# Last value tiles stored behind the next loads, their splits cut in threes, the last two steps taken product by product

## The chip, the core and the metric

The kernel runs on one core of a Trainium2 chip. The metric is device time in microseconds (us), the median of several runs. Engines: PE is TensorE (matmuls), DVE is VectorE, ACT is ScalarE, POOL is GpSimd, SP is SyncE, which here issues every DMA. Each engine works through its own list in order; it waits where an operand is not there yet, and all that stands behind in its list waits with it.

## What is computed

A chain of three parts. Attention over inputs of shape (4, 8, 576, 64), one branch downsampled by four and one masked to a band of width seven, added. Then two dense blocks over 2304 tokens. The second of these is what the change touches:

```python
def _moe2_ref(x, w_gate, w_val, w_out):     # (2304,512) x (512,1536), twice; then (1536,512)
    gate = 1.0 / (1.0 + np.exp(-(x @ w_gate)))
    val = x @ w_val
    return (gate * val @ w_out).astype(np.float32)
```

## The kernel before

Every fp32 product is three matmuls (`mm3`, lines 292 to 294): each operand is split in a high part, a copy rounded to the matmul type that ACT makes (`copy`, line 302), and a low part, the rest that DVE makes by a subtraction. The matmuls are high x high, high x low (of the moving operand), low (of the weight) x high. Tokens go in six chunks of 384, taken as three pairs p. Matrix products of the second block are made by a seven-product scheme on 2 x 2 quarters (`PRODUCTS`, `order_b`): seven matmul products on sums and differences of quarters instead of eight.

**The stage that ends at about 797 us** (lines 1180 to 1206) runs over six column groups j, three pairs p and two sides (side 0 the gate, side 1 the value). After each product PE goes on and `ends_of` lets ACT copy (`one`, `two`, `three`) and DVE add PSUM banks into tiles `c`; DVE then multiplies value by gate (line 1024). The product u goes to memory as seven forms (`u_sums`, lines 987 to 1007): b11 and the tile `low` (b21, b22) by two stores that SP issues at once (997, 998), and four differences that POOL subtracts (line 1000), stored by `stores()` some ticks later. A tick is a step of the program that lays the instructions out; a deferred call is written into the lists that many ticks later, so ticks set the order in each engine's list, and data decides when it runs.

**The last stage** (lines 1243 to 1269) makes six passes, each over six steps i; a step takes seven products of u forms by output weight forms, 21 matmuls. Its data come back from memory: u forms by `u_fetch` (line 1074), weights by `w_fetch` (1051). During the last column group (j = 5) three generators, `first_w`, `first_u` and `first_splits`, already fetch what the first pass needs, into tiles as the value stage lets them go: u forms in `pieces` of one to five forms of 384 columns, and they split them (`u_hi` on ACT, `u_lo` on DVE, line 1080; `w_hi`, `w_lo`, line 1059, for weights). How fast these splits are laid out between the value stage's own work is set by `rate` (credit per tick, line 1187) and by the price that a generator yields (line 1178). Names in rows: `x<-u` and `f<-u` are loads of u forms into tiles freed by the value stage, `f<-o` the weights of steps 4 and 5, `o<-o` weights of other steps, `u<-u` the eight last u forms, `u<-c` and `u<-t` stores of the value tiles and their differences.

**The end of a pass** is `out_ends` (line 1219): ACT copies the first sum, DVE adds the six others (line 981) into four tiles, and each finished tile goes out by a store (`put`, line 1227); in the last pass the last tile goes out in two halves.

Of the kernel before, what the change touches and what calls it, by code (L numbers as in the profile page):

```python
# [33 lines left out]
N = 384  # L34
# [6 lines left out]
NJ = F2 // 2  # L41
# [23 lines left out]
def tile_kernel(ctx: ExitStack, tc: tile.TileContext, qk, vp, v, w1, w2, mask, ident, out):  # L65
# [52 lines left out]
    def defer(n, fn, *args):  # L118
        events.setdefault(now[0] + n, []).append((fn, args))
# [10 lines left out]
    def run_later(kind=None, age=0):  # L130
        for x in list(waiting):
            if now[0] >= x[0] + age and kind in (None, x[1]):
                waiting.remove(x)
                x[2]()
# [7 lines left out]
    def run_chains(todo):  # L142
        while todo:
            for g in list(todo):
                if next(g, True):
                    todo.remove(g)

    def tick():
        now[0] += 1
        run_chains(chains.pop(now[0], []))  # L150
        todo = events.get(now[0], [])
        while todo:
            fn, args = todo.pop(0)
            fn(*args)
        events.pop(now[0], None)
        run_later(age=8)
        if beat[0]:
            beat[0]()
        lanes_step()

    lanes, credit, rate = [], [0.0], [0.0]

    def lanes_step():

        credit[0] = min(credit[0] + rate[0], 1.5)
        busy = True
        while lanes and credit[0] > 0 and busy:
            busy = False
            for lane in list(lanes):
                if lane[1] is not None and not lane[1]():  # L170
                    continue
                lane[1] = None
                got = next(lane[0], None)
                if got is None:
                    lanes.remove(lane)
                elif callable(got):
                    lane[1] = got
                else:
                    credit[0] -= got
                busy = True  # L180
                if credit[0] <= 0:
                    break

    def lane(g):
        lanes.append([g, None])

    def after(n):
        at = now[0] + n
        return lambda: now[0] >= at
# [101 lines left out]
    def mm3(o, wh, wl, xh, xl, first, last, **kw):  # L291
        nc.tensor.matmul(out=o, lhsT=wh, rhs=xh, start=first, stop=False, **kw)  # L292
        nc.tensor.matmul(out=o, lhsT=wh, rhs=xl, start=False, stop=False, **kw)  # L293
        nc.tensor.matmul(out=o, lhsT=wl, rhs=xh, start=False, stop=last, **kw)  # L294
# [6 lines left out]
    def copy(dst, src):  # L301
        nc.scalar.activation(out=dst, in_=src, func=ACTF.Copy)  # L302
# [5 lines left out]
    def store(dst, src):  # L308
        nc.sync.dma_start(out=dst, in_=src)
# [447 lines left out]
    while any(((1, 0), k) not in xt for k in range(KD)):  # L757
        keep_warm(2)
        if started[0] < n_first:
            x = items[started[0]]  # L760
# [226 lines left out]
    def u_sums(j, p, top, low, last, after_copy):  # L987
        if after_copy:
            nc.gpsimd.tensor_copy(out=spare_sb, in_=mark[after_copy][:, :1])

        if 2 in formed:
            t1, t2, t3 = (wpools["xs"].tile([128, N], F32, tag="xs", name="t") for _ in range(3))
        else:
            t1, t2, t3 = gates[0][:, 0, :], gates[0][:, 1, :], gates[1][:, 0, :]
        b11, b12, b21, b22 = top[:, 0, :], top[:, 1, :], low[:, 0, :], low[:, 1, :]
        to = ud[p][:, j]
        store(to[:, 0, :], b11)
        store(to[:, 1:3, :], low)
        for out, a, b in ((t1, b12, b11), (t3, b22, b12), (t2, b22, t1), (b12, b21, t2)):
            nc.gpsimd.tensor_tensor(out=out, in0=a, in1=b, op=ALU.subtract)  # L1000

        def stores():
            for at, t in ((3, t1), (5, t3), (4, t2), (6, b12)):
                store(to[:, at, :], t)
            summed_u.add((j, p))

        defer(4 if last else 1, stores)
# [35 lines left out]
    w_sets, u_forms, groups, w_room = {}, {}, [], {}  # L1043
# [9 lines left out]
    def w_hi(key):  # L1053
        t = w_room[key]
        copy(t[:, 0], t[:, 1].bitcast(F32))
# [6 lines left out]
    def pieces(i):  # L1062

        n, todo, at = 7 * i, 7, 0
        for g in list(groups):
            size = g[0].shape[1]
            if n < size and todo:
                k = min(size - n, todo)
                yield at, [x[:, n:n + k, :] for x in g]
                at, todo, n = at + k, todo - k, size  # L1070
            n -= size

    def u_fetch(p, i, at, t):
        nc.sync.dma_start(out=t[1].bitcast(F32), in_=ud[p][:, i, at:at + t[1].shape[1], :])

    def u_hi(t):
        copy(t[0], t[1].bitcast(F32))
# [79 lines left out]
    def first_splits():  # L1157

        p = 0
        done = set()  # L1160
        while len(u_forms) < 7 * NJ or len(fetched_w) < 8 or any(("w", x) not in done for x in fetched_w):
            ready = [(t, "u", x) for x, t in fetched_u.items() if ("u", x) not in done]
            ready += [(t, "w", x) for x, t in fetched_w.items() if ("w", x) not in done]
            ready = [x for x in ready if now[0] >= x[0] + 6]
            if not ready:
                yield after(1)
                continue
            _, kind, x = min(ready)
            done.add((kind, x))
            if kind == "w":  # L1170
                w_hi(x)
                defer(2, w_lo, x)
                yield 1.05
            else:
                t = dict(pieces(x[0]))[x[1]]
                u_hi(t)
                defer(2, u_lo, p, *x, t)
                yield 0.2 + 0.4 * t[0].shape[1]

    for j in range(NJ):  # L1180
        for p in range(len(PAIRS)):
            cycle[:] = now[0], p
            for side in range(2):
                while (j, side) not in form or p not in formed:
                    rate[0] = 0.9
                    tick()
                rate[0] = 1.0 if j == NJ - 1 else 0.4 if side else 0.65
                w = form[j, side]
                ends = ends_of(j, side, p)
                bank = next(ends)  # L1190
                if (j, p, side) == (NJ - 1, 0, 0):
                    for g in (first_w(), first_u(), first_splits()):
                        lane(g)
                for n, (a, b, at) in enumerate(PRODUCTS):
                    for k in range(2):
                        x = xform[p, k, b]
                        wh, wl = (w[:, i, a, 128 * k:128 * k + 128] for i in range(2))
                        mm3(
                            bank[at], wh, wl, x[:, 0, :], x[:, 1, :], n < 4 and k == 0,
                            k == 1, skip_group_check=n > 3,  # L1200
                        )
                    defer(1, next(ends))
                    tick()
                if p == len(PAIRS) - 1:
                    made.add((j, side))
                made.add((j, side, p))

    order_b = [(A11, B11), (S2, T2), (S1, T1), (S3, T3), (A12, B21), (S4, B22), (A22, T4)]
    passes = [(0, 0), (0, 1), (1, 1), (1, 0), (2, 0), (2, 1)]
# [33 lines left out]
    rate[0] = 0.9  # L1243
    for q, (p, e) in enumerate(passes):
        ends = None
        for i in range(NJ):
            while (e, i) not in w_sets or any((p, i, a) not in u_forms for a in range(7)):
                tick()
            w = w_sets[e, i]
            if i == 0:  # L1250
                banks = [sum_bank() for _ in range(7)]
            for n, (a, b) in enumerate(order_b):
                x = u_forms[p, i, b]
                mm3(banks[n][:, :N], w[:, 0, a], w[:, 1, a], *x, i == 0, i == NJ - 1)
                if i == NJ - 1:
                    ends = ends or out_ends(q, banks)
                    defer(1, next, ends)
                if n % 2 or n == 6:
                    tick()
            if q + 1 < len(passes) and q % 2 == 0 and i < 4:  # L1260
                key, wait = (1 - e, (i + 2) % NJ if q == 0 else i), 10 if q == 0 else 1
                defer(wait, w_fetch, key, w_room[e, i])
                defer(wait + 10, w_hi, key)
                defer(wait + 12, w_lo, key)
            if q % 2 and q + 1 < len(passes):
                for k, (at, t) in enumerate(pieces(i)):
                    u_fetch(p + 1, i, at, t)
                    defer(10 + k, u_hi, t)
                    defer(12 + k, u_lo, p + 1, i, at, t)
# [70 lines left out]
```

## Time and profile before

| | us |
|---|---|
| median of three runs | 942.21 (941.45 to 948.34) |
| the profiled execution | 942.37 |
| its span, first to last instruction | 940.6 |
| PE busy in it | 917.7 (98%) |
| DVE busy | 591.9 (63%) |
| ACT busy | 466.0 (50%) |
| POOL busy | 184.1 (20%) |

Between the span and the time of the execution lie 1.8 us that no instruction covers. PE is busy nearly throughout, so what a change can gain has to be sought in the short stretches in which PE stands still or steps slowly, and at the end behind its last matmul. In the timeline, a line gives start and duration, the engine and source line, what is written from what, the count of merged instructions, and in brackets the idle time before it and who ended that. Instructions of DVE and of ACT overlap their neighbours by some 0.08 us; PE's matmuls overlap by half, so PE is read by the distance from start to start.

### The profile page before, as it was taken

The numbers are of one execution on the slowest core, as the hardware profiler recorded it, in microseconds if no ns is written. First come the engines' busy times: TensorE is split into PE (matmuls) and PEld (weight loads), VectorE is DVE, ScalarE is ACT, GpSimd is POOL, SyncE is SP. The second block draws the span as 40 slices with busy tenths as digits, with TensorE's granted clock in tenths as the row PEclk, the third lists the DMA queues.
The fourth block names the chain that finished last, engine by engine and source line by source line (L and its number), as shares of the span: only waits on it lengthen the run. The fifth ranks groups of instructions, "written<-read, shape, count | busy, mean of one in ns | idle before, by whom it ended". The sixth has DMA issues, their size and how long they took to land.

```text
span 940.6 us, 16697 instructions
## 1 busy us (share of the span) xinstructions
PE 917.7 (98%) x6368; PEld 879.8 (94%) x6368; DVE 591.9 (63%) x993; ACT 466.0 (50%) x1161; POOL 184.1 (20%) x200
## 2 busy tenths in 40 slices
PE   7889999999999999999999999999999999899998
PEld 7678889999999999999999999999999999799997
DVE  6698965334433533466775587777768668668581
ACT  4767765544543544443644455353434356356440
POOL 2244130302222020000023243323132332200000
PEclk9899999999999999999999999999999999999999
DMA  8357553202223120357441225343425367887960
GB/s 299 126 184 271 181 166 115 65 29 78 91 64 90 44 74 20 132 227 266 149 143 45 93 101 176 124 166 118 157 110 174 113 210 252 279 311 250 327 204 35
DMA packets 72433, 142.50 MB, mean 152 GB/s; under 512 B 6608, under 2 KB 58400, under 8 KB 68000
## 3 DMA queue, kind: packets, MB, share of 16 engines
q1 hardware_dynamic: 72352, 141.43, 44.2%
q8 instruction: 50, 0.82, 0.4%
q14 instruction: 31, 0.25, 0.1%
HBM read 97.76 MB, written 43.65 MB: 150 GB/s over the span
## 4 chain that ended last, share of the span: by engine, by line
PE 88%; DVE 5%; DMA 3%; ACT 2%; issue 1%; SPq 0%; POOLq 0%; POOL 0%; DVEq 0%; ACTq 0%
PE acc L292 13%; PE ab L292 13%; PE acc L293 13%; PE acc L294 13%; PE ab L293 13%; PE ab L294 13%; PE ab L537 2%; PE ab L528 2%; PE ab L457 1%; PE ab L426 1%; DMA u<-c 1%; PE acc L753 1%; PE ab L374 1%; DMA raw<-in_w 1%; PE ab L408 1%; DVE w L263 1%
## 5 line engine op out<-in xcount | busy, mean ns | idle before, releaser
L305 DVE TENSOR_TENSOR t<-ab,t 128x384 f32<-128x384 f32 x94 | 52.3, 556 | 139.3 <-ACT t L655 138.8
L292 PE MATMUL ab<-x,w 128*128 128x384 f32 x376 | 131.5, 350 | 2.6 <-DVE t L305 2.5
L292 PE MATMUL acc<-g,w 128*128 128x384 f32 x384 | 133.2, 348 | 0.0
L293 PE MATMUL acc<-g,w 128*128 128x384 f32 x384 | 130.2, 339 | 0.0
L294 PE MATMUL acc<-g,w 128*128 128x384 f32 x384 | 129.9, 338 | 0.0
L294 PE MATMUL ab<-x,w 128*128 128x384 f32 x376 | 127.2, 338 | 0.1
L293 PE MATMUL ab<-x,w 128*128 128x384 f32 x376 | 127.0, 338 | 0.0
L655 ACT ACTIVATE t<-ab 128x384 f32<-128x384 f32 x94 | 46.1, 491 | 134.8 <-PE ab L294 132.6
L292 PE MATMUL ab<-x,f 128*128 128x384 f32 x261 | 88.3, 338 | 2.6 <-ACT f L302 2.6
L294 PE MATMUL ab<-x,f 128*128 128x384 f32 x261 | 88.4, 339 | 1.7 <-DVE f L1059 1.7
L292 PE MATMUL acc<-x,f 128*128 128x384 f32 x261 | 88.3, 338 | 1.2 <-DVE two L981 1.0
L293 PE MATMUL ab<-x,f 128*128 128x384 f32 x261 | 88.1, 338 | 0.0
L294 PE MATMUL acc<-x,f 128*128 128x384 f32 x261 | 87.7, 336 | 0.0
L293 PE MATMUL acc<-x,f 128*128 128x384 f32 x261 | 87.6, 336 | 0.0
L305 DVE TENSOR_TENSOR g<-t,g 128x384 fp32r<-128x384 f32 x96 | 56.1, 585 | 40.4 <-ACT g L302 38.6
L292 PEld LDWEIGHTS ab<-x,w 128*128 128x128 f32 x376 | 71.1, 189 | 5.5 <-DVE t L305 2.8
L292 PEld LDWEIGHTS acc<-g,w 128*128 128x128 f32 x384 | 72.5, 189 | 2.2 <-issue 1.2
L293 PEld LDWEIGHTS acc<-g,w 128*128 128x128 f32 x384 | 72.7, 189 | 0.6 <-issue 0.4
L302 ACT ACTIVATE g<-t 128x384 fp32r<-128x384 f32 x96 | 50.1, 523 | 46.1 <-DVE t L305 46.0
L294 PEld LDWEIGHTS acc<-g,w 128*128 128x128 f32 x384 | 72.6, 189 | 0.1
L294 PEld LDWEIGHTS ab<-x,w 128*128 128x128 f32 x376 | 71.1, 189 | 0.6 <-DVE w L263 0.5
L293 PEld LDWEIGHTS ab<-x,w 128*128 128x128 f32 x376 | 71.2, 189 | 0.1
(186 smaller groups left out, 2038.6 us busy)
## 6 DMA issues: line engine op xcount, KB each, us to landing
raw<-in_w SPq DMA_DIRECT2D x34, 1024.0 KB
u<-t SPq DMA_DIRECT2D x51, 192.0 KB
qk<-in_qk SPq DMA_DIRECT2D x16, 576.0 KB
x<-u SPq DMA_DIRECT2D x9, 960.0 KB
o<-o SPq DMA_DIRECT2D x18, 448.0 KB
u<-c SPq DMA_DIRECT2D x39, 192.0 KB
u<-c SPq DMA_DIRECT2D x18, 384.0 KB
o<-f SPq DMA_DIRECT2D x6, 896.0 KB
```

The lines of the kernel that those rows point to most:

```text
L263: nc.vector.tensor_tensor(out=t[:, 1, :], in0=w32, in1=t[:, 0, :].bitcast(F32), op=ALU.subtract)
L292: nc.tensor.matmul(out=o, lhsT=wh, rhs=xh, start=first, stop=False, **kw)
L293: nc.tensor.matmul(out=o, lhsT=wh, rhs=xl, start=False, stop=False, **kw)
L294: nc.tensor.matmul(out=o, lhsT=wl, rhs=xh, start=False, stop=last, **kw)
L302: nc.scalar.activation(out=dst, in_=src, func=ACTF.Copy)
L305: nc.vector.tensor_tensor(out=dst, in0=a, in1=b, op=ALU.subtract)
L374: nc.tensor.matmul(out=sd[t][o0:o0 + 64, at, :], lhsT=qd[r0:r0 + 64, 40 * j:40 * j + 64], rhs=kd[r0:r0 + 64, :], start=True, stop=True,)
L408: nc.tensor.transpose(out=tb[:, 128 * j:128 * j + 128], in_=pd[:, j, 72 * f:72 * f + 72], identity=id_sb)
L426: nc.tensor.matmul(out=ob[64 * h:64 * h + 64, :], lhsT=vd[:, f, 64 * h:64 * h + 64], rhs=pdt[:, f, h].rearrange("p j k -> p (j k)"), start ...
L528: nc.tensor.transpose(out=tb[:, j, :], in_=pl[:, 3 * f + j, :], identity=id_sb)
L537: nc.tensor.matmul(out=ob[r0:r0 + 64, QB * x:QB * x + QB], lhsT=vw[0][:, j - n, i, r0:r0 + 64], rhs=pt[:, x, o0:o0 + 64], start=True, stop ...
L655: nc.scalar.activation(out=t, in_=hb[:, :N], func=ACTF.Tanh)
```

## The change

```diff
@@ u_sums
         to = ud[p][:, j]
-        store(to[:, 0, :], b11)
-        store(to[:, 1:3, :], low)
+        if not last:
+            store(to[:, 0, :], b11)
+            store(to[:, 1:3, :], low)
 ...
         def stores():
+            if last:
+                store(to[:, 0, :], b11)
+                store(to[:, 1:3, :], low)
             for at, t in ((3, t1), (5, t3), (4, t2), (6, b12)):
                 store(to[:, at, :], t)
@@ first_splits
-                t = dict(pieces(x[0]))[x[1]]
-                u_hi(t)
-                defer(2, u_lo, p, *x, t)
-                yield 0.2 + 0.4 * t[0].shape[1]
+                whole = dict(pieces(x[0]))[x[1]]
+                size = whole[0].shape[1]
+                for a in range(0, size, 3):
+                    t = [y[:, a:min(a + 3, size), :] for y in whole]
+                    u_hi(t)
+                    defer(2, u_lo, p, x[0], x[1] + a, t)
+                    yield 0.1 + 0.45 * t[0].shape[1]
@@ the loop over j, p, side
-                rate[0] = 1.0 if j == NJ - 1 else 0.4 if side else 0.65
+                rate[0] = (0.6 if side else 0.9) if j == NJ - 1 else 0.4 if side else 0.65
@@ the last stage
-        for i in range(NJ):
-            while (e, i) not in w_sets or any((p, i, a) not in u_forms for a in range(7)):
-                tick()
-            w = w_sets[e, i]
+        for i in range(NJ if q < len(passes) - 1 else NJ - 1):
+            both = (i, i + 1) if (q, i) == (len(passes) - 1, NJ - 2) else (i,)
+            for m in both:
+                while (e, m) not in w_sets or any((p, m, a) not in u_forms for a in range(7)):
+                    tick()
 ...
             for n, (a, b) in enumerate(order_b):
-                x = u_forms[p, i, b]
-                mm3(banks[n][:, :N], w[:, 0, a], w[:, 1, a], *x, i == 0, i == NJ - 1)
-                if i == NJ - 1:
+                for m in both:
+                    x, w = u_forms[p, m, b], w_sets[e, m]
+                    mm3(banks[n][:, :N], w[:, 0, a], w[:, 1, a], *x, m == 0, m == NJ - 1)
+                if both[-1] == NJ - 1:
```

On SP, at the passage from the value stage to the last stage, the list before stands first and that of the changed kernel below it (`u_92` to `u_94` are the stored u of the three pairs; `o_99` and `o_100` the weights of steps 4 and 5):

```order
L1074 DMA f<-u_92 128x4x384
L309 DMA u_94<-c 128x384
L309 DMA u_94<-c 128x768
L1074 DMA x<-u_92 128x384 x2
L1074 DMA x<-u_92 128x5x384
L1051 DMA f<-o_99 128x896
L1051 DMA f<-o_100 128x896
L309 DMA u_94<-t 128x384 x3
L309 DMA u_94<-c 128x384
L1074 DMA u<-u_92 128x384 x8
```

```order
L1078 DMA f<-u_92 128x4x384
L1078 DMA x<-u_92 128x384 x2
L1078 DMA x<-u_92 128x5x384
L1055 DMA f<-o_99 128x896
L1055 DMA f<-o_100 128x896
L309 DMA u_94<-c 128x384
L309 DMA u_94<-c 128x768
L309 DMA u_94<-t 128x384 x3
L309 DMA u_94<-c 128x384
L1078 DMA u<-u_92 128x384 x8
```

Two stores have moved behind five loads; nothing else on SP has changed.

On DVE, in the last value side (j = 5, p = 2, side 1), before and then changed; `two<-acc` is the addition that frees a PSUM bank for PE, `c<-c 128x768` the multiplication by the gate, and x, o and f are the splits:

```order
L1080 TENSOR_TENSOR x_8455<-x_8455 128x5x384
L981 TENSOR_TENSOR two_8527<-acc_8522,two_8527 128x384
L981 TENSOR_TENSOR c_8524<-acc_8523,one_8526 128x384
L981 TENSOR_TENSOR c_8525<-acc_8520,two_8527 128x384
L1080 TENSOR_TENSOR x_5894<-x_5894 128x384
L1080 TENSOR_TENSOR x_5894<-x_5894 128x2x384
L981 TENSOR_TENSOR c_8524<-acc_8521,three_8528 128x384
L1059 TENSOR_TENSOR o_8451<-o_8451 128x896
L1024 TENSOR_TENSOR c_8524<-c_8524,c_8438 128x768
L981 TENSOR_TENSOR c_8525<-acc_8522,three_8528 128x384
L1059 TENSOR_TENSOR o_8451<-o_8451 128x896
L1024 TENSOR_TENSOR c_8525<-c_8525,c_8439 128x768
```

```order
L981 TENSOR_TENSOR two_8530<-acc_8525,two_8530 128x384
L1084 TENSOR_TENSOR x_8457<-x_8457 128x3x384
L981 TENSOR_TENSOR c_8527<-acc_8526,one_8529 128x384
L981 TENSOR_TENSOR c_8528<-acc_8523,two_8530 128x384
L981 TENSOR_TENSOR c_8527<-acc_8524,three_8531 128x384
L1084 TENSOR_TENSOR x_8457<-x_8457 128x2x384
L1028 TENSOR_TENSOR c_8527<-c_8527,c_8440 128x768
L981 TENSOR_TENSOR c_8528<-acc_8525,three_8531 128x384
L1084 TENSOR_TENSOR x_5894<-x_5894 128x384
L1028 TENSOR_TENSOR c_8528<-c_8528,c_8441 128x768
L1084 TENSOR_TENSOR x_5894<-x_5894 128x2x384
L1063 TENSOR_TENSOR o_8453<-o_8453 128x896 x2
```

The addition `two` now stands ahead of the split of five forms, of which three and then two follow, and both multiplications stand ahead of both o splits. On ACT the copies `two` and `three` have moved ahead in the same way: where a split of one form and one of five stood between `one` and `two`, only one of one form does now.

On PE, the first of the three matmuls of each product in the last two steps of the last pass, from the end of the first product of step 4, before and then changed (`acc` and `ab` with their numbers are the PSUM banks, the numbers of u tell the forms of step 5 apart):

```order
L292 MATMUL ab_9566<-x_5894,o_8451 128x384
...
L292 MATMUL acc_9567<-x_8627,o_8451 128x384
...
L292 MATMUL acc_9568<-x_8627,o_8451 128x384
...
L292 MATMUL acc_9569<-x_8627,o_8451 128x384
...
L292 MATMUL acc_9570<-x_8627,o_8451 128x384
```

```order
L292 MATMUL ab_9576<-x_5894,o_8453 128x384
...
L292 MATMUL ab_9576<-u_8667,o_8453 128x384
...
L292 MATMUL acc_9577<-x_8611,o_8453 128x384
...
L292 MATMUL acc_9577<-u_8671,o_8453 128x384
...
L292 MATMUL acc_9578<-x_8611,o_8453 128x384
```

Each bank now gets its product of step 5 right behind that of step 4, so the seven sums are finished six matmuls apart; before, they were finished three matmuls apart, all in step 5. The number of matmuls is the same. ACT and DVE each have a few more instructions from the cut pieces (five pieces of four or five forms become ten).

## Rows read from the trace of the kernel before

**Rows 1.** Waits of PE, 785 to 941 us: total, times, longest.

```profile
PE ab L292 <- ACT f L302: 2.6, 1, 2.6
PE ab L294 <- DVE f L1059: 1.7, 1, 1.7
PE acc L292 <- DVE two L981: 1.0, 1, 1.0
PE ab L292 <- DVE c L981: 0.8, 2, 0.4
```

**Rows 2.** Timeline of PE: start, duration, line, operation.

```profile
792.75 0.34 PE L294 MATMUL acc<-x,f 128*128 128x384 f32 x1
...
796.79 0.34 PE L292 MATMUL ab<-x,o 128*128 128x384 f32 x1
...
811.17 0.34 PE L294 MATMUL acc<-x,o 128*128 128x384 f32 x1
...
819.49 0.34 PE L294 MATMUL ab<-x,f 128*128 128x384 f32 x1
...
825.84 0.34 PE L294 MATMUL ab<-x,o 128*128 128x384 f32 x1
...
828.95 0.34 PE L292 MATMUL acc<-x,o 128*128 128x384 f32 x1
...
935.67 0.34 PE L294 MATMUL ab<-u,o 128*128 128x384 f32 x1
```

**Rows 3.** Windows: length, then PE, PEld, DVE, ACT, POOL, clock, DMA share, GB/s.

```profile
789.70:816.40 26.70, 21.19 (x118) 19.91 (x116) 18.27 (x20) 12.82 (x17) 5.48 (x4) 0.99 0.63 214
789.70:826.00 36.30, 30.71 (x164) 29.20 (x162) 25.51 (x31) 19.81 (x29) 5.48 (x4) 0.95 0.71 251
...
816.50:819.20 2.70, 2.70 (x9) 2.70 (x10) 2.49 (x5) 2.10 (x5) 0.00 (x0) 0.50 1.07 381
```

**Rows 4.** Timeline of SP: start and duration of the DMA issues.

```profile
800.21 3.23 SPq L309 DMA_DIRECT2D u<-c  x2
803.53 2.78 SPq L1074 DMA_DIRECT2D x<-u  x3
806.40 0.95 SPq L1051 DMA_DIRECT2D f<-o  x2
...
809.51 7.84 SPq L1074 DMA_DIRECT2D u<-u  x8
```

**Rows 5.** Timeline of ACT, splits of u forms.

```profile
790.72 2.21 ACT L302 ACTIVATE x<-x 128x384 fp32r<-128x384 f32 x2
...
811.42 1.80 ACT L302 ACTIVATE x<-x 128x1920 fp32r<-128x1920 f32 x1 [2.08 <-DMA x<-u]
```

**Rows 6.** Timeline of DVE, splits and the first pass's additions.

```profile
815.33 2.09 DVE L1059 TENSOR_TENSOR f<-f 128x896 fp32r<-128x896 f32 x2
817.62 4.11 DVE L1080 TENSOR_TENSOR u<-u 128x384 fp32r<-128x384 f32 x8 [0.20 <-ACT u L302]
...
825.99 2.27 DVE L981 TENSOR_TENSOR c<-ab,c 128x384 f32<-128x384 f32 x4
```

**Rows 7.** Timelines of DVE and POOL, where both work at once.

```profile
639.39 0.41 DVE L857 TENSOR_TENSOR raw<-raw 128x256 f32<-128x256 f32 x1
...
640.14 2.18 POOL L1000 TENSOR_TENSOR t<-c 128x384 f32<-128x384 f32 x2
...
640.19 2.40 DVE L857 TENSOR_TENSOR raw<-raw 128x256 f32<-128x256 f32 x2
...
800.26 1.02 POOL L1000 TENSOR_TENSOR t<-c 128x384 f32<-128x384 f32 x1 [11.96 <-DVE c L1024]
...
800.57 1.65 DVE L1059 TENSOR_TENSOR o<-o 128x896 fp32r<-128x896 f32 x1
```

**Rows 8.** Timelines of DVE and SP at the end.

```profile
936.45 1.08 DVE L981 TENSOR_TENSOR c<-ab,c 128x384 f32<-128x384 f32 x3
...
936.10 2.30 SPq L309 DMA_DIRECT2D out<-c  x5
```

## Prediction

> **What bounds the kernel now.** The first view is the list of PE's waits behind the point where the change begins. Four rows [rows 1]: 2.6 us for the high part of the tile f, 1.7 us for its low part, 1.0 us for the addition `two`, twice 0.4 us for additions of the first pass. No other wait there is as long as any of these; else PE goes at its own pace.
>
> The second view is PE's timeline, for what these waits cost from start to start. Its pace: the first pass's steps 0 to 3 are 84 matmuls, and the first and the last of them start 14.38 us apart [rows 2], 83 steps of 0.1733 us. Against that:
> - 792.75 to 796.79, the end of the value stage: 13 steps, 4.04 us where 2.25 would do. Lost: 1.8.
> - 811.17 to 819.49, step 4 of the first pass: 12 steps, 8.32 where 2.08 would do. Lost: 6.2. More than the two waits of 4.3, since behind them PE's granted clock is 0.50 (the lower of its levels of 1.2 and 2.4 GHz) in the window from 816.5 [rows 3]: the steps take nearly double.
> - 825.84 to 828.95, the passage to the second pass: 10 steps, 3.11 where 1.73 would do. Lost: 1.4.
>
> Together 9.4 us. Next, who causes them. SP's timeline [rows 4] shows the two stores u<-c issued at 800.21 and, by the row's length, up to 803.44; behind them, at 803.53, the three loads x<-u, and at 806.40 the two of f. The stores wait for the multiplications by the gate; the loads had to stand behind. ACT gets the load of five forms at 811.42 after an idle wait for it [rows 5], and f after that. So the 6.2 us are a queue: five loads behind two stores that wait. The 1.8 us are ACT's row at 790.72 [rows 5]: a split of one form and one of five take 2.21 us, and the copy `two`, for which PE's bank waits, stands behind them; DVE's `two` stands behind the same five forms.
>
> **The change part by part.**
>
> *The stores behind the loads.* The loads go to tiles that the value stage reads until its last matmuls. PE's last value matmul starts just ahead of 796.79 [rows 2], about 795.0 without the 1.8 us. So the five loads can be issued by about 796 instead of 803.53 to 807.35, some 8 to 11 us sooner. They carry 2.3 MB (seven forms of 128 x 384 and two tiles of 128 x 896, four bytes each); at the 381 GB/s of the busy window [rows 3] that is 6 us, so f is there at about 802 to 804. Step 4 would start at 811.17 + 0.17 - 1.8 = 809.5 and needs f's low part at its third matmul, 809.9. The load is no longer what is late. The moved stores cost nothing: they wait for the multiplications as before, and those come sooner. The u<-u loads behind them stand after POOL's last difference, some 3 us sooner than at 809.51 [rows 4], and into DMA engines that are no longer full.
>
> *What is late next: DVE.* Its list is now without the long pauses for loads. From 789.70 to 816.40, the end of f's low part, DVE is busy 18.27 of 26.70 us [rows 3]. Packed, this work ends at:
> - start 789.45 instead of 789.74: ACT's first split is three forms instead of four, and a form costs ACT at most 0.36 us (1.80 for five [rows 5]);
> - plus 18.27;
> - plus 0.4 for four more instructions by then: two of 896 columns take 2.09 us and eight of 384 take 4.11 [rows 6], 1.05 and 0.51 each, hence 1.04 ns a column and 0.1 us fixed;
> - plus about 0.65 for two short pauses for ACT, whose copies now stand between the splits (my estimate);
> - plus what POOL takes, below.
>
> *POOL's four subtractions.* Now one of them meets DVE's splits: it holds 1.02 us from 800.26, and DVE's split of o beside it takes 1.65 instead of 1.05 [rows 7]. The others find DVE paused or waiting. An earlier place shows what happens when DVE has work all the time: two subtractions of 256 columns, 0.41 us alone, take 2.40 together, while POOL's row of two subtractions runs, 2.18 instead of twice 1.02 [rows 7]; the two engines take turns, and DVE loses a POOL instruction each time. With both multiplications early and x, o, f splits queued behind, all four subtractions fall among them. Bounds: nothing beyond the 0.6 of today, or four times 1.02, 3.5 more. I take 3.1, since the first starts while DVE adds from PSUM, where no loss shows.
>
> The Trainium skill, "SBUF — State Buffer", section "Who interferes with whom", says that a DVE instruction with two SBUF inputs contends with a GpSimd instruction that reads SBUF, as an exclusive lock, and that issue order decides who waits. Read as DVE always being first, the loss would be zero and the sum 931.9; this trace's row at 640.19 shows turns instead, so I keep the rows' price.
>
> So f's low part is ready at 789.45 + 18.27 + 0.4 + 0.65 + 3.1 = 811.9, against 809.9 needed: of the 6.2 us, and of the 1.8 before it, 2.0 come back as waits on DVE (some of it perhaps already in steps 2 and 3, whose splits stand in the same list). PE then stands too short for a lower clock by anything this trace shows: the waits at 792 to 796 [rows 2] left no slow steps behind them.
>
> *The passage to the second pass.* DVE's additions start at 825.99 [rows 6] and PE is back at pace at 828.95, 3.0 us later. Packed, they start at 789.45 + 25.51 [rows 3] + 0.4 + 0.65 + 3.1 = 819.1. PE is back at pace at 822.1 instead of 828.95: 6.9 us sooner. From PE's own side it would be 9.4 - 2.0 = 7.4; the later holds, so 6.9.
>
> *The cut in threes and the rates* have no other effect on PE: the wait of 1.8 us goes, as `two` on ACT stands behind 0.5 us of splits instead of 2.21. It is worth nothing of its own while DVE is late in step 4; it only takes the place of that wait.
>
> *The last two steps by product.* PE ends as before, at 936.0 [rows 2]. Now three additions start at 936.45, the last two of half size, ending at 937.53, and five stores of 0.46 us each are issued from 936.10 to 938.40 [rows 8]. With sums finished 1.04 us apart instead of 0.52, DVE's additions of about 0.5 us keep up, and three of the stores are issued before PE ends. Left behind it: two half additions, to about 936.8, and two stores, the last issued by 937.4. That is 1.0 us. Bounds: 0.7 (the additions alone) and 1.4 (three stores).
>
> **Sum.** 6.9 + 1.0 = 7.9 us. 942.37 - 7.9 = 934.5 us, made against the profiled execution, which lies 0.16 above the median.
>
> **Rivals.**
> - *POOL costs DVE nothing more, or the data wait hides it.* DVE's additions would start at 816.0, PE would lose nothing any more: 9.4 + 1.0, 931.9 us. For it: the turns are seen with short DVE instructions only; the needs of steps 2 and 3 leave room. Against: the row of 1.65. Chance 0.25, with what lies between.
> - *The loads stay late.* The trace never shows when their tiles are free, only that they are at 803.53. If not sooner, they gain only the 0.6 MB of the two stores, 1.6 us of DMA time; with 0.5 of the passage and 1.0 at the end 3.1 us, 939.3. With half of it, 937. For it: SP works in order, and one tile that is let go late holds all five, and now also the stores. Against: PE, the last reader by the program, is done at about 795. Chance 0.17 for 936.5 and above.
> - *Slower.* POOL's four subtractions hold DVE longer than 1.02 us each. DVE's loss decides: at 3.4 us for each, 13.6 in all instead of 3.7, PE is back at pace 3.0 us later than now (6.9 less 9.9), which with 1.0 gained at the end gives 944.4; from 3.0 us each it is slower than before. Against: no row shows POOL holding more than 1.02. Chance 0.03.
> - The forecast, 933.0 to 936.5: 0.55.
>
> A measurement of this kernel can tell about 1%, 9.4 us, from no change; that is 932.8. The first rival lies mostly beyond, the forecast ends just short of it: faster 0.25, within 1% 0.73, slower 0.02. The range that holds 8 in 10 goes from 931.5, the first rival with the upper bound at the end, to 937.5.
>
> **What would show it.** Right: SP issues x<-u and f<-o at about 794 to 797; PE has no wait of over 0.5 us before 797; DVE stands without a pause from 790 to 819 with o and f splits of 1.6 to 2.1 us beside POOL's rows; PE waits about 2 us in steps 2 to 4 for low parts (o, f, x, by DVE), no window there at clock 0.50; the last store is issued about 1 us sooner after PE's end. Wrong: loads still issued behind 800; splits of their plain length beside POOL (then 932); or a wait of 2 us and more on f's load.

## The result, and the profile after

The changed kernel takes 934.36 us (median of seven runs, 932.91 to 938.72) against 941.51 for the kernel before in runs beside it (seven, 940.33 to 948.34). The ratio is 0.9919, 95% interval 0.99 to 0.9938: 7.15 us, within 1% of no change. The profiled execution took 934.36 too, its span 932.6 us.

Two distances carry the comparison below, since the work ahead of the change takes another time from run to run. The **stretch** goes from the matmul 13 ahead of the last stage's first one to PE's last matmul, start to start: before, 792.75 to 935.67 [rows 2], 142.92 us. The **tail** goes from the end of PE's last matmul to the end of the span: before, 936.01 to 940.6, 4.6 us.

From the page of the changed kernel (busy time, share of the span, count):

```profile
PE 914.5 (98%) x6368; PEld 877.5 (94%) x6368; DVE 594.2 (64%) x998; ACT 466.7 (50%) x1166; POOL 186.0 (20%) x200
```

PE's waits from 780 to 941 us (total, times, longest), which answer to [rows 1]:

```profile
PE ab L294 <- DVE f L1063: 0.8, 1, 0.8
PE ab L292 <- DVE c L981: 0.7, 2, 0.3
```

The waits for f's high part and for the addition `two` are gone. Of the 6.1 us of [rows 1], 1.5 are left. PE's timeline shows what they cost, from start to start, as in [rows 2]:

```profile
792.99 0.34 PE L294 MATMUL acc<-x,f 128*128 128x384 f32 x1
...
795.23 0.34 PE L292 MATMUL ab<-x,o 128*128 128x384 f32 x1
...
809.97 0.34 PE L293 MATMUL ab<-x,f 128*128 128x384 f32 x1
811.13 0.44 PE L294 MATMUL ab<-x,f 128*128 128x384 f32 x1 [0.83 <-DVE f L1063]
...
819.11 0.34 PE L294 MATMUL ab<-x,o 128*128 128x384 f32 x1
819.76 0.44 PE L292 MATMUL ab<-x,o 128*128 128x384 f32 x1 [0.32 <-DVE c L981]
...
928.83 0.34 PE L294 MATMUL ab<-u,o 128*128 128x384 f32 x1
```

The end of the value stage is at pace (13 steps in 2.24 us). Step 4 has one gap of 1.16, at the third matmul, 1.0 above a step. The passage to the second pass has two of 0.65, and loses 1.3 in all with smaller ones. Lost together: 2.3 of the 9.4 of before. The stretch is 135.84 us, 7.08 shorter. The tail is 932.6 - 929.17 = 3.4, 1.2 shorter. The stretch starts 0.24 later than before, so the span is 8.0 shorter.

Windows (columns as in [rows 3]); the last is the one in which the granted clock was 0.50 before:

```profile
789.40:816.00 26.60, 25.77 (x149) 25.45 (x148) 25.70 (x32) 17.63 (x29) 6.29 (x4) 1.00 0.92 320
805.70:810.60 4.90, 4.60 (x27) 4.28 (x25) 4.90 (x7) 0.77 (x2) 0.00 (x0) 1.00 0.77 242
809.50:817.40 7.90, 7.07 (x41) 6.75 (x40) 6.80 (x12) 5.30 (x10) 0.00 (x0) 1.00 0.96 324
...
816.50:819.20 2.70, 2.70 (x17) 2.62 (x15) 2.15 (x3) 2.54 (x4) 0.00 (x0) 1.00 0.94 377
```

DVE is now busy 25.70 of 26.60 us where it was 18.27 of 26.70, and the clock stays at 1.00. The two short windows are those in which SP issues the eight u<-u loads, now and before. The second in the kernel before:

```profile
809.50:817.40 7.90, 3.56 (x17) 2.92 (x16) 4.58 (x4) 3.93 (x4) 0.00 (x0) 0.91 1.03 351
```

SP's timeline, against [rows 4]:

```profile
791.20 4.09 SPq L1078 DMA_DIRECT2D x<-u  x3
795.43 0.90 SPq L1055 DMA_DIRECT2D f<-o  x2
797.54 2.71 SPq L309 DMA_DIRECT2D u<-c  x2
...
805.34 0.32 SPq L309 DMA_DIRECT2D u<-c  x1
805.71 4.86 SPq L1078 DMA_DIRECT2D u<-u  x8
810.62 2.95 SPq L1055 DMA_DIRECT2D o<-o  x5
```

The five loads start 11 to 12 us sooner. The store at 805.34 is that of POOL's last difference, and the u<-u and o<-o loads stand behind it.

DVE's timeline, with POOL's beside it:

```profile
793.02 1.36 DVE L1084 TENSOR_TENSOR x<-x 128x1152 fp32r<-128x1152 f32 x1 [0.41 <-ACT x L302]
...
797.90 1.14 DVE L1084 TENSOR_TENSOR x<-x 128x384 fp32r<-128x384 f32 x1
...
800.70 3.74 DVE L1063 TENSOR_TENSOR o<-o 128x896 fp32r<-128x896 f32 x2
804.36 2.65 DVE L1084 TENSOR_TENSOR f<-f 128x1152 fp32r<-128x1152 f32 x2
...
810.00 2.08 DVE L1063 TENSOR_TENSOR f<-f 128x896 fp32r<-128x896 f32 x2
...
817.02 2.21 DVE L1063 TENSOR_TENSOR o<-o 128x896 fp32r<-128x896 f32 x2 [0.96 <-ACT o L302]
819.15 2.27 DVE L981 TENSOR_TENSOR c<-ab,c 128x384 f32<-128x384 f32 x4
```

```profile
797.59 1.03 POOL L1001 TENSOR_TENSOR t<-c 128x384 f32<-128x384 f32 x1 [9.04 <-DVE c L1028]
799.98 1.67 POOL L1001 TENSOR_TENSOR t<-c 128x384 f32<-128x384 f32 x1 [1.36 <-DVE c L1028]
801.61 1.87 POOL L1001 TENSOR_TENSOR t<-c,t 128x384 f32<-128x384 f32 x1
803.56 1.76 POOL L1001 TENSOR_TENSOR c<-c,t 128x384 f32<-128x384 f32 x1
```

Beside POOL's rows, two o splits take 3.74 instead of the 2.09 that two of 896 columns take alone [rows 6], and POOL's own instructions 1.7 to 1.9 instead of 1.0. But ahead of the additions at 819.15, DVE stands still for 0.96 us; ACT shows why:

```profile
816.04 0.95 ACT L302 ACTIVATE o<-o 128x896 fp32r<-128x896 f32 x1 [0.57 <-DMA o<-o]
```

ACT waits there for the load of o, DVE for ACT, the additions stand behind DVE's o splits, and PE needs the additions for its banks.

The end, DVE and SP, against [rows 8]:

```profile
927.23 3.17 SPq L309 DMA_DIRECT2D out<-c  x5
...
929.20 0.62 DVE L981 TENSOR_TENSOR c<-ab,c 128x192 f32<-128x192 f32 x2 [0.50 <-PE ab L294]
```

Behind PE's last matmul only the two half additions are left.

### The profile page after: what moved, and what is told of

The parts are those of the page before. It is cut to its first block, busy times and chain, and to the rows that moved or that the text cites. A ratio compares the mean times of both kernels' runs of the same rounds, so it can differ in the third digit from the quotient of the medians.

```text
span 932.6 us, 16709 instructions
## 1 busy us (share of the span) xinstructions
PE 914.5 (98%) x6368; PEld 877.5 (94%) x6368; DVE 594.2 (64%) x998; ACT 466.7 (50%) x1166; POOL 186.0 (20%) x200
## 4 chain that ended last, share of the span: by engine, by line
PE 82%; issue 5%; DVE 5%; DMA 4%; ACT 3%; POOL 1%; SPq 0%; POOLq 0%; DVEq 0%
PE ab L292 13%; PE acc L292 12%; PE ab L294 12%; PE ab L293 12%; PE acc L293 12%; PE acc L294 12%; PE ab L537 2%; PE ab L528 1%; DMA raw<-in_w 1%; PE ab L457 1%; PE ab L426 1%; DVE w L263 1%; PE ab L408 1%; DVE raw L248 1%; PE acc L753 1%
```

## The experiments

All times are medians beside runs of the kernel before on the same chip. Gain is what the stretch of the profiled execution is shorter than 142.92; the times the stretch starts at, 789.61 to 793.34 us in these runs, show how much the work ahead of it moves a whole time. Each stretch is read from one execution; the two kernels whose stretches should be equal, before and only the last two steps, differ by 0.06 us.

| kernel | us | ratio, 95% interval | stretch | gain | tail |
|---|---|---|---|---|---|
| before | 940.61 to 942.01 | | 142.92 | | 4.6 |
| the change | 934.36 | 0.9919 (0.99 to 0.9938) | 135.84 | 7.1 | 3.4 |
| only the stores moved | 937.08 | 0.9958 (0.9942 to 0.9975) | 138.37 | 4.6 | 4.6 |
| only the cut and the rates | 935.72 | 0.9939 (0.9918 to 0.9959) | 136.14 | 6.8 | 4.2 |
| only the cut | 935.72 | 0.9948 (0.9926 to 0.997) | 137.04 | 5.9 | 4.2 |
| cut and rates, loads held behind the stores | 938.95 | 0.9979 (0.9957 to 1.0) | 140.79 | 2.1 | 4.2 |
| only the last two steps | 941.29 | 0.9997 (0.9977 to 1.0016) | 142.98 | -0.1 | 3.4 |
| the change, rate of before | 936.15 | 0.9924 (0.9892 to 0.9956) | 138.07 | 4.9 | 3.4 |
| the change, POOL fills instead of subtracting | 931.45 | 0.9896 (0.9879 to 0.9914) | 134.12 | 8.8 | 3.9 |
| the change, o loads sooner | 931.35 | 0.9884 (0.9858 to 0.9909) | 134.89 | 8.0 | 3.4 |
| the change, subtractions on DVE | 930.77 | 0.9883 (0.9852 to 0.9914) | 133.96 | 9.0 | 3.4 |
| both of these | 932.34 | 0.9894 (0.9868 to 0.992) | 134.19 | 8.7 | 3.4 |
| subtractions on DVE, one o split later | 931.15 | 0.9897 (0.987 to 0.9924) | 133.52 | 9.4 | 3.4 |

### Only the stores moved

The cut in threes, the rates and the last two steps are as before. Against the changed kernel (the last two steps are not shown):

```diff
-                rate[0] = (0.6 if side else 0.9) if j == NJ - 1 else ...
+                rate[0] = 1.0 if j == NJ - 1 else ...
-                for a in range(0, size, 3):
...
+                u_hi(t)
+                defer(2, u_lo, p, *x, t)
+                yield 0.2 + 0.4 * t[0].shape[1]
```

> Only the two stores are moved; pieces, rates and the last two steps are as before. My theory: the wait at the end of the value stage (1.8 us) stays, the loads of x and f are issued at about 795 to 798, the long wait in step 4 with its slow clock (6.2 us) goes, f's low part is ready near 811 to 812. What is late next is the passage to the second pass, since POOL's last subtraction still ends near 808 and the u and o loads behind it start no sooner than before: PE back at pace some 4 to 5 us sooner, about 937.5 us. Rival, parts add: 6.2 us of gain, 936. Rival, the stores alone are worth little because DVE's list is as long as before: under 1.5 us of gain, 941.

The gain is 4.6 us. The longest of PE's waits from 780 to 941 us, and SP's loads:

```profile
PE acc L292 <- DVE two L981: 1.0, 1, 1.0
```

```profile
786.88 6.85 SPq L1078 DMA_DIRECT2D x<-u  x3
793.87 0.90 SPq L1055 DMA_DIRECT2D f<-o  x2
797.11 3.24 SPq L309 DMA_DIRECT2D u<-c  x2
```

The wait at the end of the value stage stays, and with it the 1.8 us; the waits for f in step 4 are gone. So this edit takes away the queue in front of the loads. It gains less than the 6.2 us of step 4, since step 5 and the passage now lose 3.1 us where the passage lost 1.4: the u<-u loads come only 0.9 us sooner in the stretch, 15.9 us from its start (805.52 - 789.64) instead of 16.8.

### Only the cut and the rates

The stores stand where they stood before, and the last two steps are as before. Against the changed kernel:

```diff
-        if not last:
-            store(to[:, 0, :], b11)
-            store(to[:, 1:3, :], low)
+        store(to[:, 0, :], b11)
+        store(to[:, 1:3, :], low)
```

> Only the cut in threes and the rates; stores and last steps as before. My theory: the wait at the end of the value stage goes; both multiplications come about 3 us sooner, so the two stores are issued at about 797.5 and 800 and the five loads from 800.4 instead of 803.5; step 4 still waits, about 3 us less, with less or no slow clock: about 938 us. Rival, the cut is worth only its own wait of 1.8 us: 940.5. Rival, all of it is swallowed by step 4's wait for loads: 942.

The gain is 6.8, more than expected, and nearly that of the whole change. SP's timeline says how:

```profile
789.67 4.68 SPq L1074 DMA_DIRECT2D x<-u  x3
796.61 2.71 SPq L309 DMA_DIRECT2D u<-c  x2
799.42 0.91 SPq L1051 DMA_DIRECT2D f<-o  x2
```

The three x loads went ahead of the two stores, though the stores were not moved. The program lays SP's list out tick by tick; with the pieces cut and repriced, the generator of the loads gets to them some ticks sooner, and they are written into the list first. Of the five loads only f<-o stays behind, and since the multiplications also come sooner, it is issued at 799.42 instead of 806.40 [rows 4].

### The cut and the rates, with the loads held behind the stores

This asks which of the two did it: the order on SP, or the sooner multiplications. `issued` is set where the two stores are issued, and the generator of the x loads waits for it. Against the run with only the cut and the rates:

```diff
+        issued[0] = last
...
-            yield lambda: (NJ - 1, side, q) in made and (q == 0 or not holds[0])
+            yield lambda: ... and ((q, side) != (2, 1) or issued[0])
```

> The cut in threes and the rates, with the loads of x held back until the two stores are written into SP's list: SP then has the order of the kernel before, the stores ahead of all five loads. It asks whether the cut alone gained because the x loads had moved ahead of the stores by themselves, or because the multiplications, and with them the stores, come 3 us sooner. Theory, sooner stores: x is issued at about 3 us behind the first multiplication pair, near 799 to 800 instead of 803.5, f near 802.5; f's low part is 1 to 2 us later than with the cut alone, and of its 7.0 us some 5 to 6 stay: 937 us. Rival, the order on SP: the long wait in step 4 with the slow clock comes back, 3 us of gain or less, 939 or later.

The gain falls to 2.1. SP's and PE's timelines:

```profile
796.81 2.71 SPq L309 DMA_DIRECT2D u<-c  x2
799.61 1.44 SPq L1076 DMA_DIRECT2D x<-u  x3
```

```profile
810.95 0.44 PE L292 MATMUL ab<-x,f 128*128 128x384 f32 x1 [1.73 <-ACT f L302]
...
812.64 0.45 PE L294 MATMUL ab<-x,f 128*128 128x384 f32 x1 [1.07 <-DVE f L1061]
```

The multiplications stay 3 us sooner (stores at 796.81 instead of 800.21 [rows 4]), yet both waits for f are back. Of the 6.8 us, 4.7 hang on the place of the x loads on SP: 2.2 of them in step 4, the others in step 5 and at the passage, whose o loads are issued at 813.90 instead of 809.67. The 2.1 left are about the value stage's 1.8. This is the rival's time, but the slow clock that the rival brings did not come back: the granted clock is 1.00 from 805.20 to 820.00.

### Only the cut, at the rate of before

Against the run with only the cut and the rates:

```diff
-                rate[0] = (0.6 if side else 0.9) if j == NJ - 1 else ...
+                rate[0] = 1.0 if j == NJ - 1 else ...
```

> The cut in threes alone, at the old rate of 1.0; stores and last steps as before. On SP x is ahead of the two stores, f behind them. DVE takes more splits ahead of the multiplications than with the new rates. Theory: PE has no wait ahead of 797 us; the multiplications and stores come about 1 us later than with the new rates; from the last value side to PE's end 2 us more than with the cut and the rates, as between the changed kernel and the one with the old rate: 937.5 us. Rival: the rates are worth nothing without the moved stores, 935.7.

The gain is 5.9: with the stores unmoved, the rates are worth 0.9 us of the stretch and the cut the rest. The expected 937.5 did not come; in whole time, 935.72 with and without the rates, the rival's 935.7 did, so that the 0.9 rests on the two stretches. On SP the x loads stand ahead of the two stores here too, so the cut alone moves them.

### The whole change at the rate of before

> The changed kernel with the old rate of 1.0 in the last column group; cut, stores and last steps as changed. On SP nothing differs; on DVE one split of o moves ahead of the second multiplication and small splits move between the additions. My theory: PE's waits stay those of the changed kernel (1.0 us in step 4, 1.1 at the passage), within 0.5 us: 934.5. Rival, the rates are what frees DVE's additions: a wait near 795 us comes back and the multiplications, stores and u loads are 1 us later, 935.5.

The edit is the same line. The gain falls from 7.1 to 4.9, so the rates are worth 2.2 us here, where I had expected less than 0.5. The gap in step 4 is 1.16 us in both; what grew are the gaps at the passage to the second pass, which are five of 0.41 to 0.98 instead of two of 0.65. The rows show a way for it, counted from the start of the stretch: with the old rate DVE's second multiplication starts at 7.84 instead of 5.97, POOL's last difference ends at 14.05 instead of 12.33, and ACT's first o split of the passage, behind its load, starts at 25.25 instead of 23.05, 2.2 us later. No run had the old rate with the o loads sooner, so this cause is read and not tested. As the whole times of this kernel and of the change overlap, the 2.2 rests on the two stretches.

### Only the last two steps by product

> Only the last two steps product by product. My theory: nothing changes before the last pass; the last store is issued about 1.0 to 1.2 us sooner behind PE's last matmul, 3.4 us instead of 4.6 from PE's end to the end of the span: about 940.5 us. Rival, the end is bound by the data of the stores (0.8 MB at some 350 GB/s takes 2.2 us) and little is gained: 0.4 us or less.

Everything else is as before. The stretch is unchanged (142.98), the tail 3.44 instead of 4.59: 1.2 us gained. The whole time's interval, 0.9977 to 1.0016, can't show that; the tail can.

### POOL fills instead of subtracting

```diff
-            nc.gpsimd.tensor_tensor(out=out, in0=a, in1=b, op=ALU.subtract)
+            if last:
+                nc.gpsimd.memset(out, 0.0)
+            else:
+                nc.gpsimd.tensor_tensor(out=out, in0=a, in1=b, op=ALU.subtract)
```

> The changed kernel, with POOL's four subtractions of the last value tiles replaced by four fills with zero, which read nothing; these four of the 126 stored forms are then wrong. My theory: DVE's splits beside them (x 1.14, o 1.90 and 1.91, f 2.18 in the changed kernel) fall back to 0.55, 1.08, 1.08 and 1.36; f's low part is ready 2.5 to 3 us sooner and PE has no wait in step 4 (1.0 us); the u and o loads also start sooner (POOL's last ends near 801 instead of 805.3), so the passage's 1.1 to 1.4 us shrink: about 932.5 us. Rival, the long splits are DMA or SBUF traffic and not POOL: durations stay, 934.4 us.

The gain is 8.8, 1.7 more than the change. DVE and POOL:

```profile
792.24 1.36 DVE L1087 TENSOR_TENSOR x<-x 128x1152 fp32r<-128x1152 f32 x1 [0.41 <-ACT x L302]
...
799.32 2.08 DVE L1066 TENSOR_TENSOR o<-o 128x896 fp32r<-128x896 f32 x2
```

```profile
792.32 1.14 POOL L1002 MEMSET t<- 128x384 f32 x3 [4.55 <-DMA u<-t]
```

DVE's splits have their plain length again, 2.08 for two of o, and PE has no gap in step 4 any more. The split at 792.24 takes 1.36 us with three of POOL's fills beside it, as long as the same split of the changed kernel (793.02) without: these fills, which only write, cost DVE nothing. The Trainium skill, "SBUF — State Buffer", section "Who interferes with whom", says that a DVE instruction with two SBUF inputs contends with a GpSimd instruction that reads SBUF and not with one that only writes it; these rows agree, with 3.74 beside reads and 1.36 unchanged beside writes. Fills also end sooner, so that what waits for POOL's results comes sooner; that part is not separated here. The o and f splits have no fill beside them, so for these the run shows only that their extra length goes with POOL's subtractions.

### The loads of o sooner

The passage waited for ACT's o split, and that for its load. Here two of the five o loads are issued behind f<-o instead of behind u<-u; the splits keep their order.

```diff
-            (lambda: (5, 6) in fetched_u, "b", 6),
+            (lambda: (4, 1) in fetched_u, "b", 6),
-            fetched_w[key] = now[0]
+            fetched_w[key] = now[0] + (8 if key[0] else 0)
```

> The changed kernel with the two weight loads of the second pass's first steps issued right behind the two loads of f instead of behind the eight u loads; DVE's and ACT's lists stay. My theory, the passage waits for these loads and not for DVE: DVE's pause of 1.0 us ahead of its o split and PE's waits of 0.3 twice at the passage go, 933.4 us. Rival, the 0.9 MB ahead of the stores delay the u loads, which PE needs in step 5: the wait moves there, 934.4 or later.

PE's one wait from 780 to 941 us, and DVE's o splits at the passage:

```profile
PE ab L294 <- DVE f L1063: 0.8, 1, 0.8
```

```profile
812.82 2.10 DVE L1063 TENSOR_TENSOR o<-o 128x896 fp32r<-128x896 f32 x2 [0.28 <-ACT o L302]
```

The waits at the passage are gone, none has come in step 5, the one in step 4 is as it was, and the gain is 8.0: 0.9 more than the change. So the passage was bound by the loads of o, not by the length of DVE's list.

### The last subtractions on DVE

```diff
-            nc.gpsimd.tensor_tensor(out=out, in0=a, in1=b, op=ALU.subtract)
+            (nc.vector if last else nc.gpsimd).tensor_tensor(out=out, in0=a, in1=b, op=ALU.subtract)
```

> The changed kernel with the four subtractions of the last value tiles made by DVE behind its split of two forms, instead of by POOL. My theory: four subtractions cost DVE about 4 x 0.48 = 1.9 us where POOL's turns cost it 3.05, so f's low part is 1 us sooner and step 4's wait of 1.0 goes; the last difference is there at about 803 instead of 805.3, the u and o loads 2 us sooner, and the passage's waits shrink: 932.5 us. Rival, DVE is the bound and the work moved to it costs more than the turns: f's low part later, 935 to 936.

The gain is 9.0, 1.9 more than the change. DVE's and SP's timelines:

```profile
797.37 1.02 DVE L1001 TENSOR_TENSOR t<-c 128x384 f32<-128x384 f32 x2
798.30 0.55 DVE L1001 TENSOR_TENSOR t<-c,t 128x384 f32<-128x384 f32 x1
798.89 0.56 DVE L1001 TENSOR_TENSOR c<-c,t 128x384 f32<-128x384 f32 x1
799.37 2.09 DVE L1063 TENSOR_TENSOR o<-o 128x896 fp32r<-128x896 f32 x2
801.37 1.82 DVE L1084 TENSOR_TENSOR f<-f 128x1152 fp32r<-128x1152 f32 x2
```

```profile
800.26 5.36 SPq L1078 DMA_DIRECT2D u<-u  x8
```

Four subtractions take DVE 2.0 us (797.37 to 799.37). Made by POOL they cost DVE 3.1: the x split 1.14 instead of 0.55 (a plain split of 384 columns), 3.74 instead of 2.09, 2.65 instead of 1.82. So DVE saves a microsecond by doing POOL's work itself. The u<-u loads, counted from the start of the stretch, come 2.7 us sooner (800.26 - 790.24 = 10.0, against 805.71 - 792.99 = 12.7), and the o loads behind them too: both waits that the change left are gone. One new gap of 0.57 comes in step 2, where o's low part now stands behind the subtractions.

### Both

> Both of the former together: early weight loads and the four subtractions on DVE. My theory: no wait of PE above 0.3 us is left from the last value side to the end: 2.1 us less than the changed kernel, 932.0 us. Rival, the DMA engines are full from 794 to 816 and the loads that are sooner make others later: no better than the better of the two.

The gain is 8.7, more than with the o loads sooner alone and less than with the subtractions on DVE alone. The gap of 0.57 in step 2 stays, and with two o loads ahead of the stores the u loads come later again.

### The subtractions on DVE, one o split later

On top of the edit that gives the subtractions to DVE:

```diff
-                        defer(1 if last else 4, u_sums, j, p, c[0], c[1], last, None)
+                        defer(3 if last else 4, u_sums, j, p, c[0], c[1], last, None)
-        defer(4 if last else 1, stores)
+        defer(2 if last else 1, stores)
```

> The changed kernel with the four subtractions on DVE, standing one split of o later than in the run with the subtractions on DVE. Theory: that run's one wait of PE of 0.4 us in step 2, for that split of o, goes; nothing else: 930.5 us. Rival: the differences, stores and u loads are 1 us later and step 5 or the passage waits instead, 931 or later.

The stretch is the shortest, 133.52, gain 9.4, with no gap in PE's steps above 0.21 us: all that the prediction counted as lost. In whole time, 931.15 cannot be told from the 930.77 of the kernel it was made from. In the stretch both beat the change, by 2.3 and 1.9 us. In whole time their ratios to the kernel before are 0.9897 and 0.9883 where the change has 0.9919, but the intervals overlap.

## Why the prediction came out, step by step

**The sum.** Predicted: 6.9 us up to the second pass and 1.0 at the end. Measured: 7.1 in the stretch and 1.2 in the tail. The forecast of 934.5 stands beside 934.36. That closeness is better than its reasons: POOL's share was taken 0.6 us too long and a wait of 1.0 us for the o load was not seen, and the two nearly cancel. The starting point helped too: 7.9 was taken off 942.37, which is 0.86 above the median of the seven runs, while stretch and tail together are 8.3 shorter and the medians 7.15. A slip of the sum changes nothing: 942.37 less 9.4 and 1.0 is 932.0, where 931.9 stands.

**The queue on SP: right.** Loads predicted by about 796, issued at 791.20 to 795.90; f's load is no longer waited for. The run with the loads held behind the stores shows that the x loads' place in this queue was worth 4.7 us; the run with the stores alone gains 4.6.

**The lower clock: right.** With no long wait ahead, 816.5 to 819.2 runs at 1.00 instead of 0.50.

**The wait for `two` at the value stage's end: right.** It goes with the cut (1.8 us) and stays without it.

**DVE becomes late: right in place, half in size.** f's low part was forecast for 811.9 and is there at 811.1; PE waits 1.0 instead of 2.0. The mis-sized term is POOL's: I took 3.1 us on top of the 0.6 of before, 3.7 in all; it is 3.1 in all. The smaller price stood in the row that I read: at 640.19 [rows 7] two subtractions take 2.40 instead of twice 0.41, 0.8 for each turn and not 1.02. That they take turns is right: the run with fills and the run with the subtractions on DVE give back DVE's plain lengths and remove this wait.

**The passage: right time, wrong cause.** The additions start at 819.15, predicted 819.1, as the end of a packed list on DVE. DVE was not packed there. It waited 0.96 us for the load of o, which stood on SP behind the u loads, and those behind the store of POOL's last difference. The step that failed is the list taken as packed up to 819.1, with 0.65 us of short pauses for ACT as its only waits: the o loads were left out of the sum. "Some 3 us sooner" for the u<-u loads was right, they came 3.8 us sooner (805.71 for 809.51). "Into DMA engines that are no longer full" held while SP issued them (DMA share 0.77 instead of 1.03) and not behind that, where the o loads follow: 0.96 from 809.50 to 817.40. The run with the o loads sooner shows the cause. That 819.15 meets 819.1 is luck: the 0.6 us that POOL did not take and the wait that I did not see nearly cancel.

**The cut in threes "is worth nothing of its own": wrong.** Alone it is worth 5.9 us, with its rates 6.8. I had read the order of SP's list for the full change only, where nothing but the two stores seems to move, and so put the whole of the queue down to the stores. In fact either edit alone takes the x loads out from behind the stores; f<-o is moved by the stores' edit only. On top of the cut and the rates, moving the stores brings 0.3 us (7.1 against 6.8). On top of the moved stores, the cut and the rates bring 2.5 (7.1 against 4.6), 1.8 of them the wait that they were meant for.

**The rates "have no other effect on PE": wrong.** By the stretches they are worth 0.9 us without the moved stores and 2.2 with them, where by the rows they make the multiplications, and with them the loads of o, sooner.

**The end: right.** 1.2 against 1.0, shown alone in the run with only this edit. Tails of 4.2 in three kernels without this edit, instead of 4.6, and of 3.9 in the one with fills stay unexplained.

**The rivals.** That POOL costs nothing did not come: the rows beside it are long. That the loads stay late did not come. The run with the loads held behind the stores is no test of it, though the numbers meet: it gains 2.1 us in the stretch, as this rival does (3.1 without the 1.0 at the end), but the rival's 2.1 are DMA time and the passage, the run's are the value stage. Nothing pointed to slower, but its sentence "no row shows POOL holding more than 1.02" is a misreading. Rows of POOL and DVE in the kernel before:

```profile
803.17 2.47 POOL L1000 TENSOR_TENSOR t<-c 128x384 f32<-128x384 f32 x1 [1.89 <-DVE c L1024]
```

```profile
803.01 1.75 DVE L1080 TENSOR_TENSOR f<-f 128x1536 fp32r<-128x1536 f32 x1
```

POOL's second subtraction there did meet a split of DVE, and took 2.47 us. The split took 1.75, about what 1536 columns cost alone (1.70 at the 1.04 ns and 0.1 us of [rows 6]): POOL came second and waited, and DVE lost nothing.

## What to carry to other kernels

When an in-order issuer of DMAs has a store that waits for a result, look at every load behind it in the list: here loads behind two stores cost 4.6 to 4.7 us, and the order changed with an edit that did not name them. Where several edits are made together, print the order of the lists for each of them alone before giving a gain to one. A few small operations given to POOL to relieve DVE can cost DVE more than making them (3.1 against 2.0 us here), once DVE has work all the time.

## What the runs showed of the hardware

DVE and POOL, both with two operands in SBUF, take turns instruction by instruction when both have work waiting, and both pay: DVE's 896-column subtraction takes about 1.9 us instead of 1.05, POOL's 384-column one 1.7 to 1.9 instead of 1.0. I had expected DVE to lose a whole POOL instruction of 1.0 us each time; it loses about 0.8. Where only one instruction of each met in the kernel before, the later one paid alone: DVE at 800.57 (1.65 [rows 7]), POOL at 803.17 (2.47).

The length of an issue row on SP went with how full the DMA engines were: eight u<-u loads take SP 7.84 us before [rows 4] at a DMA share of 1.03, and 4.86 after at 0.77. In the kernel before, three of these issues stand 1.3, 0.8 and 1.6 us for x<-u and f<-o loads that are eight places ahead of them in SP's list. This reads as if SP goes on only when the eighth DMA before has landed; whether the program's semaphores or the chip set that, no run tested.
